# A chunked attention's scores and weighted sums in 64-row by 64-column tiles of TensorE, with its first loads in another order

## The chip, the cores and the metric

One core of one Trainium2 chip runs the whole kernel. The metric is the device time of one execution in microseconds (us). The core's engines are named as the profile names them: PE (TensorE matmuls), PEld (TensorE weight loads, which overlap PE), DVE (VectorE), ACT (ScalarE), POOL (GpSimd) and SP (SyncE, which here only issues transfers).

## The reference

Attention inside chunks of 64 tokens (8 batches, 8 heads, 576 tokens, 64 dimensions a head), then two stages over the 4608 tokens by 512 columns that come out: a mixture of 8 experts of which each token takes one, and a dense two-layer block. All data are float32.

```python
scores = scale * np.matmul(q_c, k_c.transpose(0, 1, 2, 4, 3))   # chunks of 64 tokens
scores = scores - np.max(scores, axis=-1, keepdims=True)
attn = np.exp(scores)
attn = attn / (np.sum(attn, axis=-1, keepdims=True) + 1e-09)
out = np.matmul(attn, v_c)
...
expert_idx = np.argmax(logits, axis=1)                          # logits = x @ w_gate
h = np.maximum(xe @ w1[e], 0.0)
out[mask] = gate_w[mask, None] * (h @ w2[e])
...
h = np.maximum(x @ w_in, 0.0)
return h * h @ w_out
```

## The kernel before

Three stages follow one another on PE: attention(), experts() and second(). The change is in attention() alone.

Attention works on 36 units of 128 tokens (two chunks of 64). A loop over `it` from -4 to 36 is software-pipelined, and everything is issued in the order in which it is written; each engine runs its own instructions in that order. In one iteration stand, for units that lie one to four apart: scores(it+1), the transposes of half of a q or k tile (trans, first half), x_t (transposes an older result), expo(it+1), trans (second half), pv(it-1), attn_t(it), and in some iterations the steps that choose the expert of each token: gate, gate_t with route, place, scatter, one in each of four iterations in turn.

- trans: PE turns q (even iterations) or k (odd ones) into PSUM tiles `tq`, and ACT copies them out in eight pieces of 64 partitions (four for each half) into `qT` or `kb`. The head's 64 dimensions lie on 64 partitions, so two heads (j = 0 and 1) fill 128. Before the change `kb` holds, for each pair of heads and each chunk, 2 x 64 columns: head 0's keys on partitions 0 to 63 in the first 64 columns, head 1's on partitions 64 to 127 in the last 64, and zeros elsewhere, written once at the start (fill_k, DVE).
- scores: eight matmuls (four pairs of heads, two chunks c2), each with 128 rows, 64 columns of weights (`lhsT`) and 128 moving columns, half of which meet the zeros. The two chunks write PSUM partitions 0 to 63 and 64 to 127. DVE then takes the maximum (`mx`) and subtracts it (`at`); ACT exponentiates (expo).
- attn_t transposes `at` on PE (`ta`), and ACT copies it out (`aT`). pv multiplies by v: again eight matmuls with 128 rows, 64 weight columns, and 130 moving columns of `vb`, which holds v of two heads side by side, with zeros and a column of ones for the sum (fill_v: on DVE for the first batch's set of buffers, on POOL for the second's). DVE divides (`rc`, `x`), and SP stores `x`.
- load_qk(u) loads q and k of two units (four chunks) on SP's queue, three u ahead of the k that has just been transposed; load_v(b) loads a batch of v on POOL's queue, for the first batch on both. A transfer on either queue waits until the transfer eight before it has landed, beside what its buffer needs.
- PSUM has eight banks: four tiles `t` that the transposes share, two score tiles `s` of a bank each, and one tile `v` of two banks.
- The buffers of tag "a" hold qk tiles (and, before, one `vb`), those of tag "b" hold kb, qT (and one `vb`), those of tag "h" the other `vb`; the experts use the same tags later for their weights.

A matmul of float32 data stands in the profile as two weight loads and two matmul records; a transpose as one of each.

Of the kernel before, what the change touches and what calls it, by code (L numbers as in the profile page):

```python
# [8 lines left out]
F32 = mybir.dt.float32  # L9
# [4 lines left out]
ALU = mybir.AluOpType  # L14
AX = mybir.AxisListType
PSUM = bass.MemoryType.PSUM
# [4 lines left out]
def kernel(ctx, tc, q, k, v, w_gate, w1, w2, w_in, w_out, out):  # L21
    nc = tc.nc
    B, H, S, D = q.shape
    NT, DM = out.shape
    NE = w_gate.shape[1]
    CH = 64
    NCB = S // CH
    NPAIR = H // 2
# [81 lines left out]
    at = const.tile([128, NI, QT], I32, name="at")  # L110
# [118 lines left out]
    def attention():  # L229
        with ExitStack() as actx:  # L230
            ps_t = actx.enter_context(tc.tile_pool(name="ps_t", bufs=4, space=PSUM))
            ps_s = actx.enter_context(tc.tile_pool(name="ps_s", bufs=2, space=PSUM))
            ps_v = actx.enter_context(tc.tile_pool(name="ps_v", bufs=1, space=PSUM))

            vb = [[tl("hhhhhhba"[4 * s + p], [128, NCB, 2, D + 1], F32, f"vb{s}{p}") for p in range(NPAIR)] for s in range(2)]
            kb = [tl("b", [128, NPAIR, 4, 2, CH], F32, f"kb{s}") for s in range(2)]
            st = {}

            def load_qk(u):
# [15 lines left out]
            def load_v(b, engs=(nc.gpsimd,), c0=0, c1=NCB):  # L255
                for p in range(NPAIR):
                    for j in range(2):
                        engs[j % len(engs)].dma_start(  # L258
                            out=vb[b % 2][p][64 * j:64 * j + 64, c0:c1, j, 0:D],
                            in_=v[b, 2 * p + j, CH * c0:CH * c1].rearrange("(c s) d -> s c d", s=CH),  # L260
                        )

            def trans(nm, u, hh):
                if hh == 0:
                    if nm == "q":
                        st["qT", u] = tl("b", [128, NPAIR, 128, 2], F32, f"qT{u}")
                src = st[nm, u] if hh == 0 else st.pop((nm, u))
                ps = ps_t.tile([128, 2, 2, 128], F32, tag="t", name="tq")
                for h in range(4):
                    nc.tensor.transpose(ps[:, h // 2, h % 2, :], src[:, 4 * hh + h, :], ident)  # L270
                for r in range(2):
                    for j in range(2):
                        i_ = ps[64 * r:64 * r + 64, :, j, :]
                        if nm == "q":
                            o = st["qT", u][64 * j:64 * j + 64, 2 * hh:2 * hh + 2, :, r]
                        else:
                            i_ = i_.rearrange("p a (c i) -> p a c i", c=4)
                            o = kb[u % 2].rearrange("p a c j (i r) -> p a j c i r", r=2)[64 * j:64 * j + 64, 2 * hh:2 * hh + 2, j, :, :, r]
                        nc.scalar.copy(o, i_)  # L279

            def scores(i):
                u, h2 = divmod(i, 2)
                qt, kt = st["qT", u], kb[u % 2]
                ps = ps_s.tile([128, H, CH], F32, tag="s", name="sc")
                for p in range(NPAIR):
                    for c2 in range(2):
                        c = 2 * h2 + c2
                        nc.tensor.matmul(
                            ps[64 * c2:64 * c2 + 64, 2 * p:2 * p + 2, :],
                            lhsT=qt[:, p, 32 * c:32 * c + 32, :].rearrange("p i r -> p (i r)"),  # L290
                            rhs=kt[:, p, c],
                            start=True,
                            stop=True,
                        )
                mx = tl("m", [128, H], F32, "mx")
                nc.vector.tensor_reduce(mx, ps, axis=AX.X, op=ALU.max)
                at = tl("r", [128, H, CH], F32, "at")
                nc.vector.tensor_tensor(out=at, in0=ps, in1=mx[:, :, None].to_broadcast([128, H, CH]), op=ALU.subtract)
                st["at", i] = at

            def expo(i):
                at = st["at", i]
                nc.scalar.activation(out=at, in_=at, func=AF.Exp, scale=scale)
# [10 lines left out]
            def pv(i):  # L314
                aT = st.pop(("aT", i))
                ps = ps_v.tile([128, 2, 512], F32, tag="v", name="pv")
                for p in range(NPAIR):
                    for c2 in range(2):
                        b, c = divmod(2 * i + c2, NCB)
                        o = (p % 2) * 2 * (D + 1)  # L320
                        nc.tensor.matmul(  # L321
                            ps[64 * c2:64 * c2 + 64, p // 2, o:o + 2 * (D + 1)],
                            lhsT=aT[:, p, 64 * c2:64 * c2 + 64],
                            rhs=vb[b % 2][p][:, c].rearrange("p j d -> p (j d)"),
                            start=True,
                            stop=True,
                        )
                pv_ = ps[:, :, 0:4 * (D + 1)].rearrange("p a (h d) -> p a h d", d=D + 1)
                rc = tl("m", [128, 2, 4, 1], F32, "rc")
                nc.vector.tensor_scalar(out=rc, in0=pv_[:, :, :, D:D + 1], scalar1=1e-9, scalar2=None, op0=ALU.add)  # L330
                nc.vector.reciprocal(out=rc, in_=rc)
                x = tl("x", [128, 2, 4, D], F32, "x")
                nc.vector.tensor_tensor(out=x, in0=pv_[:, :, :, 0:D], in1=rc.to_broadcast([128, 2, 4, D]), op=ALU.mult)
                nc.sync.dma_start(out=x_d[128 * i:128 * i + 128, :], in_=x.rearrange("p a h d -> p (a h d)"))
                st["x", i] = x

# [32 lines left out]
            nc.vector.memset(zero, 0)  # L369
            nc.scalar.dma_start(out=tk_d.rearrange("(e r) k -> e r k", e=NE)[:, 0, :], in_=zero)  # L370


            def fill_k(s):
                t = kb[s]
                nc.vector.memset(t[0:64, :, :, 1, :], 0.0)
                nc.vector.memset(t[64:128, :, :, 0, :], 0.0)

            def fill_v(s, eng):
                for t in vb[s]:
                    eng.memset(t[0:64, :, 1, :], 0.0)  # L380
                    eng.memset(t[64:128, :, 0, :], 0.0)
                    eng.memset(t[0:64, :, 0, D:D + 1], 1.0)
                    eng.memset(t[64:128, :, 1, D:D + 1], 1.0)

            fill_k(0)
            load_qk(1)
            c = min(6, NCB)
            load_v(0, (nc.gpsimd, nc.sync), 0, c)
            load_qk(2)
            if c < NCB:  # L390
                load_v(0, (nc.gpsimd, nc.sync), c)
            fill_v(1, nc.gpsimd)
            load_v(1)

            todo = {}
            for i in range(NTILE - 2):
# [6 lines left out]
            for g in range(NG - 1):  # L403
                t = 4 * g + (7 if g < NG - 3 else 6)
# [12 lines left out]
            for it in range(-4, NTILE + 1):  # L417
                u, h2 = divmod(it + 4, 2)
                tr = it + 4 < NTILE
                if 0 <= it + 1 < NTILE:  # L420
                    scores(it + 1)
                if tr:
                    trans("qk"[h2], u, 0)
                for step, i in todo.get(it, ()):
                    step(i)
                if 0 <= it + 1 < NTILE:
                    expo(it + 1)
                if tr:
                    trans("qk"[h2], u, 1)
                    if h2 == 1 and u + 3 < NUNIT:  # L430
                        load_qk(u + 3)
                if it == -4:
                    fill_k(1)
                if it == -3:
                    fill_v(0, nc.vector)
                if it == -1:
                    constants()
                if 0 <= it - 1 < NTILE:
                    pv(it - 1)
                    lo, hi = (2 * (it - 1)) // NCB, (2 * (it - 1) + 2) // NCB  # L440
                    if hi > lo and lo + 2 < B:
                        load_v(lo + 2)
                if 0 <= it < NTILE:
                    attn_t(it)
                late_steps(it)
                if it == NTILE - 14:
                    for _ in range(4):
                        load_next(most=1)
                if NTILE - 5 <= it < NTILE - 2:
                    split(1, 0, it - NTILE + 5, eng=nc.gpsimd)  # L450
# [599 lines left out]
    with tc.manual_schedule():  # L1050
        attention()
        experts()
        second()
# [30 lines left out]
```

## Time and profile before

| | |
|---|---|
| median of 3 runs | 1479.04 us (1475.89 to 1479.36) |
| the profiled execution | 1477.98 us, of which the span from first to last instruction is 1476.2 |
| PE busy | 1429.1 us, 97% of the span |
| attention, until the last weighted sum | 0 to 200 us |
| experts | to 690 us |
| second | to 1476 us |

The profiled execution lies 1.06 us under the median. PE's share is one of busy records: matmuls are pipelined and the profile models their ends, so a busy PE isn't PE at its peak. The rows further down are of one profiled execution. In a row of the timeline stand the start, the duration (both in us), the engine, the line of the kernel, what was done with which tiles and shapes and how many instructions the row merges; in brackets, how long the engine was idle before it and what ended that.

### The profile page before, as it was taken

How to read it: one execution, taken by the hardware profiler on the slowest of the kernel's cores; microseconds unless marked ns; L12 is line 12 of the kernel's file. 1: busy time of each engine (PE TensorE's matmuls, PEld its weight loads, DVE VectorE, ACT ScalarE, POOL GpSimd, SP SyncE). 2: the span in 40 equal slices, each digit the busy share in tenths (PEclk: the TensorE clock that was granted, in tenths of full speed). 3: DMA queues.
4: the chain of work that ended last, by engine and by line, in shares of the span. 5: the costliest groups of instructions: out<-in, count | busy, mean ns of one | idle time of the engine just before them, and what ended most of it. 6: DMA issues, size and time to landing. Idle time of an engine off the chain costs nothing.

```text
span 1476.2 us, 21686 instructions
## 1 busy us (share of the span) xinstructions
PE 1429.1 (97%) x8186; PEld 1219.6 (83%) x8186; DVE 757.4 (51%) x1374; ACT 601.0 (41%) x1111; POOL 468.7 (32%) x566
## 2 busy tenths in 40 slices
PE   6999978999999999999999999999999999999998
PEld 5777758888889999998888888888888888888886
DVE  4766767768887878885532232322233232322322
ACT  7988833443444445554432222222222222222222
POOL 5335455435545545653003040120403003040201
PEclk9999999999999999999999999999999999999999
DMA  9998645757767777885301010010101001010000
GB/s 202 262 216 208 171 130 183 217 171 228 235 210 232 238 229 256 260 269 179 107 1 59 0 60 0 24 36 0 59 0 52 8 8 52 1 59 1 30 2 29
DMA packets 144370, 172.91 MB, mean 117 GB/s; under 512 B 18160, under 2 KB 103872, under 8 KB 144256
## 3 DMA queue, kind: packets, MB, share of 16 engines
q1 hardware_dynamic: 110032, 112.58, 27.0%
q0 software_dynamic: 17920, 40.51, 9.8%
q10 hardware_dynamic: 16304, 18.36, 3.8%
q8 instruction: 66, 1.08, 0.3%
q14 instruction: 48, 0.39, 0.1%
HBM read 133.05 MB, written 38.34 MB: 116 GB/s over the span
## 4 chain that ended last, share of the span: by engine, by line
PE 53%; POOL 0%; POOLq 0%; issue 0%; DVE 0%
PE hp L993 27%; PE py L1014 26%; POOL out_dram L974 0%; POOLq L1079 0%; DVE o L1022 0%; POOL between L973 0%
## 5 line engine op out<-in xcount | busy, mean ns | idle before, releaser
L993 PE MATMUL hp<-xm,w_None 128*128 128x512 f32 x1728 | 416.5, 390 | 3.1 <-DVEq L937 3.1
L993 PEld LDWEIGHTS hp<-xm,w_None 128*128 128x128 f32 x1728 | 325.4, 188 | 71.0 <-ACTq L937 3.3
L1014 PE MATMUL py<-w_None,h 128*128 128x512 f32 x1512 | 363.2, 389 | 0.0
L1014 PEld LDWEIGHTS py<-w_None,h 128*128 128x128 f32 x1512 | 283.9, 188 | 58.8
L998 DVE SCALAR_TENSOR_TENSOR rs<-hp,rs 128x512 f32<-128x512 f32 x144 | 99.6, 691 | 435.0 <-ACT rs L997 431.6
L997 ACT ACTIVATE rs<-hp 128x512 f32<-128x512 f32 x144 | 85.9, 597 | 456.6 <-PE hp L993 446.0
L755 PE MATMUL pa<-xs,w 128*128 128x256 f32 (+2 forms) x1344 | 242.5, 329 | 6.9 <-DVE h L759 2.9
L767 PE MATMUL pb<-h,w 128*128 128x256 f32 (+2 forms) x1344 | 243.9, 331 | 0.0
L974 POOL DMA_INDIRECT out_dram<-o,tp x36 | 35.1, 974 | 628.6 <-ACT o L1020 622.6
L755 PEld LDWEIGHTS pa<-xs,w 128*128 128x128 f32 x1344 | 211.4, 189 | 24.7 <-DVE h L759 4.1
L767 PEld LDWEIGHTS pb<-h,w 128*128 128x128 f32 x1344 | 209.9, 190 | 14.5
L1000 DVE TENSOR_TENSOR h<-rs,h 128x512 fp32r<-128x512 f32 x144 | 99.7, 693 | 99.0 <-ACT h L999 95.5
L758 ACT ACTIVATE h<-pa 128x256 fp32r<-128x256 f32 (+2 forms) x112 | 53.2, 475 | 217.6 <-PE pa L755 169.9
L190 DVE TENSOR_TENSOR w<-raw,w 128x1024 fp32r<-128x1024 f32 x100 | 132.7, 1328 | 17.2 <-ACT w L189 12.4
L999 ACT CAST h<-rs 128x512 fp32r<-128x512 f32 x144 | 89.4, 621 | 111.2 <-DVE rs L998 100.2
L189 ACT CAST w<-raw 128x1024 fp32r<-128x1024 f32 x113 | 118.2, 1047 | 0.0
L759 DVE SCALAR_TENSOR_TENSOR h<-pa,h 128x256 fp32r<-128x256 f32 (+2 forms) x112 | 59.6, 535 | 61.5 <-ACT h L758 49.9
L803 POOL TENSOR_TENSOR cr<-cr 128x256 f32<-128x256 f32 x64 | 50.2, 784 | 124.5 <-ACT h L758 43.3
L804 POOL TENSOR_TENSOR cr<-cr 128x256 f32<-128x256 f32 x64 | 71.5, 1117 | 5.0
L258 POOL DMA_DIRECT2D vb<-in_v_dram x64 | 46.4, 747 | 67.4 <-PE pv L321 67.3
L270 PE MATMUL tq<-ident,qk 128*128 128x128 f32 x288 | 47.7, 296 | 14.1 <-DMA qk<-in_q_dram 9.9
L279 ACT COPY qT<-tq 64x256 f32<-64x256 f32 x144 | 56.0, 389 | 10.8 <-PE tq L270 9.1
(197 smaller groups left out, 1316.0 us busy)
## 6 DMA issues: line engine op xcount, KB each, us to landing
raw<-in_moe_w_dram SPq DMA_DIRECT2D x112, 512.0 KB
x_d<-x SPq DMA_DIRECT2D x36, 256.0 KB
x<-y_d POOLq DMA_DIRECT2D x36, 256.0 KB
cr<-in_moe_w_in_dram SPq DMA_DIRECT2D x32, 256.0 KB
cr<-in_moe_w_out_dram SPq DMA_DIRECT2D x32, 256.0 KB
vb<-in_v_dram POOLq DMA_DIRECT2D x56, 144.0 KB
qk<-in_q_dram SPq DMA_DIRECT2D x12, 512.0 KB
qk<-in_k_dram SPq DMA_DIRECT2D x12, 512.0 KB
```

Of the source, the lines that this page charges most:

```text
L189: nc.scalar.copy(w[0], raw)
L190: eng.tensor_tensor(out=w[1], in0=raw, in1=w[0], op=ALU.subtract)
L755: nc.tensor.matmul(ps[:, 0:N], lhsT=w[wl][:, kk, o:o + 128], rhs=xT[:, xl, kk, 0:N], start=(kk == 0 and wl + xl == 0), stop=(kk == KD - 1 ...
L759: nc.vector.scalar_tensor_tensor(out=h[:, 1, 0:N], in0=ps[:, 0:N], scalar=0.0, in1=h[:, 0, 0:N], op0=ALU.max, op1=ALU.subtract)
L767: nc.tensor.matmul(pb[d][:, 0:N], lhsT=w[wl][:, f % 2, 128 * d:128 * d + 128], rhs=h[:, hl, 0:N], start=(f + hl + wl == 0), stop=(f == NF ...
L804: nc.gpsimd.tensor_tensor(out=af, in0=af, in1=ef, op=ALU.add)
L993: nc.tensor.matmul(ps, lhsT=w[wl][:, kk, o:o + 128], rhs=xT[:, xl, kk, :], start=(kk == 0 and wl + xl == 0), stop=(kk == KD - 1 and wl == 1))
L997: nc.scalar.activation(out=rs[:, 0], in_=ps, func=AF.Relu)
L998: nc.vector.scalar_tensor_tensor(out=rs[:, 1], in0=ps, scalar=0.0, in1=rs[:, 0], op0=ALU.max, op1=ALU.mult)
L999: nc.scalar.copy(h[:, 0], rs[:, 1])
L1000: nc.vector.tensor_tensor(out=h[:, 1], in0=rs[:, 1], in1=h[:, 0], op=ALU.subtract)
L1014: nc.tensor.matmul(ys[t], lhsT=h[:, hl, 128 * t:128 * t + 128], rhs=w[wl][:, g % 2, :], start=(g == 0 and hl + wl == 0), stop=(g == NF2 - ...
```

## The change

`kb` and `vb` lose their zeros: keys and values of head j lie on partitions 64j to 64j+63 and nothing else does. Each score or weighted-sum matmul of 128 rows becomes two of 64 rows (j = 0, 1), which read 64 partitions each and write different PSUM banks, with 64 (65) moving columns instead of 128 (130). The score tile takes two banks and has one buffer where it had two of one bank. The `vb` tiles are four instead of eight and all have tag "h", so that "a" has a fourth buffer for qk and "b" a third for qT. The zero fills go; only columns of ones are written, by POOL, at the start. The first batch of v is loaded in chunks 0 to 1 and 2 to 8 (before 0 to 5 and 6 to 8), the first piece before the second q and the rest behind the third k; load_v(1) is written in iteration 0 instead of before the loop.

```diff
-            ps_s = actx.enter_context(tc.tile_pool(name="ps_s", bufs=2, space=PSUM))
+            ps_s = actx.enter_context(tc.tile_pool(name="ps_s", bufs=1, space=PSUM))
...
-            vb = [[tl("hhhhhhba"[4 * s + p], [128, NCB, 2, D + 1], F32, f"vb{s}{p}") for p in range(NPAIR)] for s in range(2)]
-            kb = [tl("b", [128, NPAIR, 4, 2, CH], F32, f"kb{s}") for s in range(2)]
+            vb = [[tl("h", [128, 2, NCB, D + 1], F32, f"vb{s}{z}") for z in range(NPAIR // 2)] for s in range(2)]
+            kb = [tl("b", [128, NPAIR, 128, 2], F32, f"kb{s}") for s in range(2)]
...
-                            out=vb[b % 2][p][64 * j:64 * j + 64, c0:c1, j, 0:D],
+                            out=vb[b % 2][p // 2][64 * j:64 * j + 64, p % 2, c0:c1, 0:D],
...
+                to = st["qT", u] if nm == "q" else kb[u % 2]
                 for r in range(2):
                     for j in range(2):
...
-                        nc.scalar.copy(o, i_)
+                        nc.scalar.copy(to[64 * j:64 * j + 64, 2 * hh:2 * hh + 2, :, r], ps[64 * r:64 * r + 64, :, j, :])
...
-                ps = ps_s.tile([128, H, CH], F32, tag="s", name="sc")
+                ps = ps_s.tile([128, 2, 512], F32, tag="s", name="sc")
                 for p in range(NPAIR):
                     for c2 in range(2):
-                        c = 2 * h2 + c2
-                        nc.tensor.matmul(
-                            ps[64 * c2:64 * c2 + 64, 2 * p:2 * p + 2, :],
-                            lhsT=qt[:, p, 32 * c:32 * c + 32, :].rearrange("p i r -> p (i r)"),
-                            rhs=kt[:, p, c],
...
+                        for j in range(2):
+                            c = slice(64 * h2 + 32 * c2, 64 * h2 + 32 * c2 + 32)
+                            nc.tensor.matmul(
+                                ps[64 * c2:64 * c2 + 64, j, CH * p:CH * p + CH],
+                                lhsT=qt[64 * j:64 * j + 64, p, c].rearrange("q i r -> q (i r)"),
+                                rhs=kt[64 * j:64 * j + 64, p, c].rearrange("q i r -> q (i r)"),
...
-                        nc.tensor.matmul(
-                            ps[64 * c2:64 * c2 + 64, p // 2, o:o + 2 * (D + 1)],
-                            lhsT=aT[:, p, 64 * c2:64 * c2 + 64],
-                            rhs=vb[b % 2][p][:, c].rearrange("p j d -> p (j d)"),
...
+                        for j in range(2):
+                            nc.tensor.matmul(
+                                ps[64 * c2:64 * c2 + 64, j, (D + 1) * p:(D + 1) * (p + 1)],
+                                lhsT=aT[64 * j:64 * j + 64, p, 64 * c2:64 * c2 + 64],
+                                rhs=vb[b % 2][p // 2][64 * j:64 * j + 64, p % 2, c],
...
-            fill_k(0)
+            for s_ in range(2):
+                for t in vb[s_]:
+                    nc.gpsimd.memset(t[:, :, :, D:D + 1], 1.0)
+            load_v(0, (nc.gpsimd, nc.sync), 0, 2)
             load_qk(1)
-            c = min(6, NCB)
-            load_v(0, (nc.gpsimd, nc.sync), 0, c)
             load_qk(2)
-            if c < NCB:
-                load_v(0, (nc.gpsimd, nc.sync), c)
-            fill_v(1, nc.gpsimd)
-            load_v(1)
+            load_v(0, (nc.gpsimd, nc.sync), 2)
...
-                if it == -4:
-                    fill_k(1)
-                if it == -3:
-                    fill_v(0, nc.vector)
+                if it == 0:
+                    load_v(1)
```

On PE, one iteration in the middle of attention before (from one call of scores to the next; `tq` is a half of trans, `tx` x_t, `ta` attn_t):

```order
L288 MATMUL sc<-kb_115,qT_1244 64x128 x8
L270 MATMUL tq<-ident,qk_1047 128x128 x4
L348 MATMUL tx<-ident,x 128x128 x4
L270 MATMUL tq<-ident,qk_1047 128x128 x4
L321 MATMUL pv<-vb_110,aT 64x130 x2
L321 MATMUL pv<-vb_111,aT 64x130 x2
L321 MATMUL pv<-vb_112,aT 64x130 x2
L321 MATMUL pv<-vb_113,aT 64x130 x2
```

and such an iteration of the changed kernel:

```order
L286 MATMUL sc<-kb_111,qT_1440 64x64 x16
L271 MATMUL tq<-ident,qk_1374 128x128 x4
L348 MATMUL tx<-ident,x 128x128 x4
L271 MATMUL tq<-ident,qk_1374 128x128 x4
L321 MATMUL pv<-vb_108,aT 64x65 x8
L321 MATMUL pv<-vb_109,aT 64x65 x8
L309 MATMUL ta<-ident,at 128x128 x4
L286 MATMUL sc<-kb_110,qT_1620 64x64 x16
```

Nothing has moved; scores and pv have sixteen matmuls of half the moving columns where they had eight.

On POOL's queue at the start, before (vb_106 to vb_109 are the first batch's buffers, vb_110 to vb_113 the second's; a DMASW semaphore tells that the transfer eight earlier has landed):

```order
L258 DMA vb_106<-in_v_dram 64x3x64
L258 DMA vb_107<-in_v_dram 64x3x64
L258 DMA vb_108<-in_v_dram 64x3x64
L258 DMA vb_109<-in_v_dram 64x3x64 [waits DMASW0_49]
L380 MEMSET vb_110 64x9x65
L381 MEMSET vb_110 64x9x65 [waits Pool_49]
...
L383 MEMSET vb_113 64x9
L258 DMA vb_110<-in_v_dram 64x9x64 [waits DMASW1_49]
```

and in the changed kernel (vb_106 and vb_107 are the first batch's, vb_108 and vb_109 the second's):

```order
L374 MEMSET vb_109 128x18
L259 DMA vb_106<-in_v_dram 64x2x64 x2
L259 DMA vb_107<-in_v_dram 64x2x64 x2
L259 DMA vb_106<-in_v_dram 64x7x64 x2
L259 DMA vb_107<-in_v_dram 64x7x64
L259 DMA vb_107<-in_v_dram 64x7x64 [waits DMASW0_49]
L259 DMA vb_108<-in_v_dram 64x9x64 [waits DMASW1_49]
L259 DMA vb_108<-in_v_dram 64x9x64 [waits DMASW2_49]
```

The second batch's loads, though written in iteration 0, stand directly behind the first batch's on POOL and wait for nothing but the transfers eight before them; sixteen memsets that stood between are gone.

## Rows read from the trace of the kernel before

**Rows 1.** The page, section 1: busy us, share of the span, instructions.

```profile
PE 1429.1 (97%) x8186; PEld 1219.6 (83%) x8186; DVE 757.4 (51%) x1374; ACT 601.0 (41%) x1111; POOL 468.7 (32%) x566
```

**Rows 2.** Windows, four stretches: each engine's busy us (instructions), PE clock, DMA share, GB/s.

```profile
0.00:12.46 12.46, 5.69 (x25) 4.71 (x25) 8.62 (x21) 7.01 (x16) 11.06 (x29) 1.00 0.93 192
12.46:35.42 22.96, 15.81 (x142) 12.84 (x141) 7.73 (x22) 17.61 (x44) 7.49 (x15) 0.85 1.20 207
35.42:186.25 150.83, 142.32 (x1598) 110.94 (x1597) 106.01 (x264) 132.14 (x307) 64.94 (x98) 1.00 0.89 213
186.25:212.00 25.75, 15.92 (x135) 11.34 (x135) 14.68 (x35) 6.60 (x11) 12.87 (x17) 0.93 0.46 140
```

**Rows 3.** Groups on ACT, 35.42 to 186 us: busy us, mean ns, idle before them.

```profile
L279 ACT COPY kb<-tq 64x256 f32<-64x256 f32 x120 | 46.7, 389 | 1.4
L279 ACT COPY qT<-tq 64x256 f32<-64x256 f32 x116 | 45.2, 390 | 5.1 <-PE tq L270 3.8
L303 ACT ACTIVATE at<-at 128x512 f32<-128x512 f32 x31 | 19.5, 631 | 5.5 <-DVE at L298 4.6 <-ACT kb L279 0.3
L311 ACT COPY aT<-ta 128x512 f32<-128x512 f32 x31 | 18.1, 585 | 3.7 <-PE tq L270 3.0
L358 ACT COPY gs<-gl 128x512 f32<-128x512 f32 x7 | 4.1, 591 | 1.2 <-PE tx L348 0.9 <-PE tq L270 0.4
```

**Rows 4.** ACT's waits, 35.42 to 186 us: us in total, times, longest.

```profile
ACT at L303 <- DVE at L298: 4.6, 6, 1.5
ACT qT L279 <- PE tq L270: 3.8, 4, 1.0
ACT aT L311 <- PE tq L270: 3.0, 2, 1.6
ACT gs L358 <- PE tx L348: 0.9, 1, 0.9
ACT gs L358 <- PE tq L270: 0.4, 1, 0.4
```

**Rows 5.** Timeline of one iteration in the middle, PE and PEld.

```profile
48.35 0.85 PEld L288 LDWEIGHTS sc<-kb,qT 128*64 128x64 f32 x16 [0.17 <-issue]
48.35 1.09 PE L288 MATMUL sc<-kb,qT 128*64 128x128 f32 x16
...
51.01 1.11 PE L321 MATMUL pv<-vb,aT 128*64 128x130 f32 x16
...
52.63 0.42 PEld L288 LDWEIGHTS sc<-kb,qT 128*64 128x64 f32 x8 [0.17 <-issue]
```

**Rows 6.** Line 356, a gate step: ns min/median/max, first and last start.

```profile
L356 PE MATMUL gl<-xT,wg x8: 592/604/617, 57.0 to 57.5; 128*32 128x512 f32 x8
```

**Rows 7.** Timeline of the start: the third k arrives, and what follows.

```profile
27.56 1.56 PE L270 MATMUL tq<-ident,qk 128*128 128x128 f32 x8 [3.40 <-DMA qk<-in_k_dram]
...
28.36 1.59 ACT L279 COPY kb<-tq 64x256 f32<-64x256 f32 x4 [2.95 <-PE tq L270]
...
33.46 1.58 ACT L279 COPY qT<-tq 64x256 f32<-64x256 f32 x4 [0.60 <-PE tq L270]
```

**Rows 8.** Groups of the start, 0 to 20 us: two of the zero fills.

```profile
L380 POOL MEMSET vb<- 64x585 f32 x4 | 2.4, 590 | 0.2
...
L375 DVE MEMSET kb<- 64x1024 f32 x2 | 1.8, 912 | 0.4 <-issue 0.4
```

**Rows 9.** Timeline of an iteration in which POOL scatters.

```profile
95.99 1.09 PE L288 MATMUL sc<-kb,qT 128*64 128x128 f32 x16
...
97.57 0.99 POOL L510 DMA_INDIRECT tk_d<-tok,pos  x1 [0.23 <-issue]
...
98.33 0.69 DVE L296 TENSOR_REDUCE mx<-sc 128x8 f32<-128x512 f32 x1 [2.68 <-PE tx L348]
...
99.08 0.38 ACT L279 COPY qT<-tq 64x256 f32<-64x256 f32 x1 [1.05 <-PE tq L270]
```

**Rows 10.** Timeline of the end of attention, DVE.

```profile
201.24 0.17 DVE L330 TENSOR_SCALAR rc<-pv 128x8 f32<-128x8 f32 x1 [4.01 <-remote]
```

More of the change, by code (lines that the diff above doesn't have):

```diff
@@ L270, in trans @@
                     nc.tensor.transpose(ps[:, h // 2, h % 2, :], src[:, 4 * hh + h, :], ident)
+                to = st["qT", u] if nm == "q" else kb[u % 2]
                 for r in range(2):
                     for j in range(2):
[L273 to L278, printed above, removed]
-                        nc.scalar.copy(o, i_)
+                        nc.scalar.copy(to[64 * j:64 * j + 64, 2 * hh:2 * hh + 2, :, r], ps[64 * r:64 * r + 64, :, j, :])
             def scores(i):
@@ L283, in scores @@
                 qt, kt = st["qT", u], kb[u % 2]
-                ps = ps_s.tile([128, H, CH], F32, tag="s", name="sc")
+                ps = ps_s.tile([128, 2, 512], F32, tag="s", name="sc")
                 for p in range(NPAIR):
                     for c2 in range(2):
-                        c = 2 * h2 + c2
-                        nc.tensor.matmul(
-                            ps[64 * c2:64 * c2 + 64, 2 * p:2 * p + 2, :],
-                            lhsT=qt[:, p, 32 * c:32 * c + 32, :].rearrange("p i r -> p (i r)"),
-                            rhs=kt[:, p, c],
[L292 to L296, printed above, removed]
+                        for j in range(2):
[4 more added lines that the diff above has]
+                                rhs=kt[64 * j:64 * j + 64, p, c].rearrange("q i r -> q (i r)"),
+                                start=True,
+                                stop=True,
+                            )
+                s4 = ps[:, :, 0:NPAIR * CH].rearrange("q j (p k) -> q j p k", k=CH)
+                mx = tl("m", [128, 2, NPAIR], F32, "mx")
+                nc.vector.tensor_reduce(mx, s4, axis=AX.X, op=ALU.max)
                 at = tl("r", [128, H, CH], F32, "at")
-                nc.vector.tensor_tensor(out=at, in0=ps, in1=mx[:, :, None].to_broadcast([128, H, CH]), op=ALU.subtract)
+                nc.vector.tensor_tensor(out=at.rearrange("q (p j) k -> q j p k", j=2), in0=s4,
+                                        in1=mx[:, :, :, None].to_broadcast([128, 2, NPAIR, CH]), op=ALU.subtract)
                 st["at", i] = at
@@ L319, in pv @@
                         b, c = divmod(2 * i + c2, NCB)
-                        o = (p % 2) * 2 * (D + 1)
-                        nc.tensor.matmul(
-                            ps[64 * c2:64 * c2 + 64, p // 2, o:o + 2 * (D + 1)],
-                            lhsT=aT[:, p, 64 * c2:64 * c2 + 64],
-                            rhs=vb[b % 2][p][:, c].rearrange("p j d -> p (j d)"),
[L325 to L328, printed above, removed]
+                        for j in range(2):
[3 more added lines that the diff above has]
+                                rhs=vb[b % 2][p // 2][64 * j:64 * j + 64, p % 2, c],
+                                start=True,
+                                stop=True,
+                            )
+                pv_ = ps[:, :, 0:4 * (D + 1)].rearrange("q j (p d) -> q j p d", d=D + 1)
                 rc = tl("m", [128, 2, 4, 1], F32, "rc")
@@ L331, in pv @@
                 nc.vector.reciprocal(out=rc, in_=rc)
-                x = tl("x", [128, 2, 4, D], F32, "x")
-                nc.vector.tensor_tensor(out=x, in0=pv_[:, :, :, 0:D], in1=rc.to_broadcast([128, 2, 4, D]), op=ALU.mult)
+                x = tl("x", [128, 4, 2, D], F32, "x")
+                nc.vector.tensor_tensor(out=x.rearrange("q p j d -> q j p d"), in0=pv_[:, :, :, 0:D], in1=rc.to_broadcast([128, 2, 4, D]), op=ALU.mult)
                 nc.sync.dma_start(out=x_d[128 * i:128 * i + 128, :], in_=x.rearrange("p a h d -> p (a h d)"))
@@ L370, in attention @@
             nc.scalar.dma_start(out=tk_d.rearrange("(e r) k -> e r k", e=NE)[:, 0, :], in_=zero)
[L373 to L383, printed above, removed]
-            fill_k(0)
+            for s_ in range(2):
+                for t in vb[s_]:
+                    nc.gpsimd.memset(t[:, :, :, D:D + 1], 1.0)
+            load_v(0, (nc.gpsimd, nc.sync), 0, 2)
             load_qk(1)
-            c = min(6, NCB)
-            load_v(0, (nc.gpsimd, nc.sync), 0, c)
             load_qk(2)
-            if c < NCB:
-                load_v(0, (nc.gpsimd, nc.sync), c)
-            fill_v(1, nc.gpsimd)
-            load_v(1)
+            load_v(0, (nc.gpsimd, nc.sync), 2)
             todo = {}
```

## The prediction

> **What bounds the kernel now.** The page comes first: PE is busy for 97% of the span [rows 1]. That is a mean over three stages, and the change lies in the first, so the second view is the table of windows over attention alone [rows 2]. It cuts attention at calls of scores: the start, until the fifth call at 35.42 us; the regular middle, 31 calls until 186.25 us; and the end, until the experts' matmuls fill PE at 212 us. The start is bound by transfers: PE is busy for 15.8 of 23.0 us, while the DMA engines' share is 1.20 at 207 GB/s. In the middle PE and ACT are both nearly full: 142.3 and 132.1 of 150.8 us. PE's figure contains modelled ends, ACT's does not, so I read the middle from ACT: an iteration takes 150.83 / 31 = 4.87 us, and ACT works in it for 132.14 / 31 = 4.26 us. The groups on ACT say with what [rows 3]: eight copies of 0.39 us, the exponential, the copy of `aT` and, in one iteration of four, `gs`. None of them gets shorter by this change.
>
> ACT is idle for 18.7 us of the middle. Its list of waits names 12.7 us of that in 14 waits [rows 4]: 8.1 us in eight that PE ended (3.8 + 3.0 + 0.9 + 0.4) and 4.6 us in six that DVE's subtraction ended, which itself follows scores. The other 6 us lie in gaps of 10 to 20 ns between instructions (18.7 less 12.7, over 307 instructions, is 20 ns each). So whatever PE saves in the middle, at most about 12.7 us can come out of the stage.
>
> **The change on PE.** A scores call now issues 16 records, whose weight loads take 0.85 us, and takes 1.09 us with its latency; pv takes 1.11 us [rows 5]. 0.85 / 8 is 106 ns for two records: the two chunks write different column halves, and their records run as a pair. That more than two can run at once is shown by the gate, with four tiles of 32 columns: its eight records of some 600 ns all start within 0.5 us, 57.0 to 57.5 [rows 6]. That is two rounds of four, the second 0.5 us or less behind the first, for 512 moving columns; the 106 ns for 128 fits the same pace. So time goes with moving columns, and tiles in different columns run together.
>
> The changed calls have 32 records each, in four tiles (two row halves, two column halves), of 64 or 65 moving columns. If all four run together, that is 8 rounds of half of 106 ns, 0.42 us instead of 0.85: 0.42 us less for each call, 0.84 us in an iteration. If the row halves don't run side by side, it is 16 rounds of 53 ns, 0.85 us as now. If in addition a record keeps the 53 ns that it has now on average, however few columns it has, 32 records take 1.70 us. No row shows two row halves at once, so both ends stay open; I take the first, since the gate shows four tiles in flight, which is the nearest row.
>
> **What that is worth, stage by stage.** *Middle.* An iteration of PE, from one scores call to the next, took 4.28 us, 48.35 to 52.63 [rows 5], near ACT's 4.26, so PE's 0.84 us is at first only a lead over ACT. It is worth something where ACT waits. Between two such waits PE does one scores and one pv, so each of the eight waits that PE ends can shrink by 0.84 us at most: four of 3.8 us in all, the longest 1.0, give 3.4; two of 3.0 give 1.7; 0.8 and 0.4 come from `gs`; together 6.3 us. The six that wait for DVE's subtraction shrink by the earlier scores alone, 0.42 us each, 2.5 us. The most is 8.8 us. The least is nothing, for a reason that the rows show (first rival, below). Between the two I take half, 4.4 us.
>
> *Start.* PE waits 3.40 us for the third k, until 27.56 us, and ACT 2.95 us behind it [rows 7]. Before that k has to come, before: three q and three k of 0.52 MB, 0.98 MB of the first v (SP's last quarter MB of v is behind it), and the second batch of v, 1.18 MB; now 0.13 MB of SP's v instead of 0.39 is ahead, the rest stands behind. The second v isn't held back: on POOL nothing stands between it and the first, it even comes earlier by the fills that are gone. So 0.26 MB less, at 207 GB/s [rows 2], is 1.25 us; the q that comes next (ACT's copies of it start at 33.46 us) has the same bytes ahead as before, and stands 0.6 us behind ACT anyway. I take 1.2 us. The most is the whole wait, 3.4 us. The least: the second v, 5.7 us of transfers at that rate, gets ahead of the second k. Then ACT has that k's copies, an exponential, the third q's copies and `aT`, some 7.5 us of work, between about 20.7 and 28.2 us, and still reaches the third k's copies at 28.4, as now: nothing lost.
>
> *End.* The last pv is done before 199 us, but DVE begins its division at 201.24 us, after 4.01 us idle, released by nothing on PE [rows 10]. Three pv calls of 0.42 us lie ahead of it; I count 0, at most 1.3 us.
>
> *What costs nothing.* The zero fills: the largest groups take 2.4 us on POOL and 1.8 on DVE [rows 8], all before 14.4 us, while PE waits for loads; without that cover they would be worth some 5 us on either engine. The fourth qk and third qT buffers only take waits from SP and ACT that end behind the transfers and PE anyway. The single score buffer adds a wait: scores must follow DVE's subtraction of the call before, and the transposes behind it on PE, whose copies ACT needs, wait too. In a regular iteration the subtraction ends some 2 us before the next scores, which hides it; where scatters run it may not (a rival).
>
> **Sum.** 4.4 + 1.2 + 0 = 5.6 us off the profiled 1477.98, 1472.4. Experts and second are PE-bound behind attention and move up whole. The profiled execution was 1.06 us under the median, so the median should come to **1473 us**; its own range is 1465 to 1477.
>
> **Rivals.** *Scatters, not PE, make ACT's waits.* In the iteration at 96 us scores ends by its record at 97.08, yet DVE's maximum starts at 98.33 after 2.68 us idle, and ACT's copy at 99.08 after 1.05, while POOL issues its indirect scatters [rows 9]. PE's signals seem to come late there, and a faster PE wouldn't release them sooner. Against it: PE would enter such a stretch with more lead. Then only the start's 1.2 us remains, 1478. Chance 0.20.
>
> *The change doesn't do what it says*: row halves take turns, a call stays 0.85 us: 1478 again. 0.07.
>
> *Everything is collected*: 8.8 + 3.4 + 1.3 = 13.5 us, 1465. 0.07.
>
> *A record costs 53 ns whatever its size* (slower). Then two calls cost 2 x 0.85 us more in an iteration, PE needs about 4.28 + 1.70, some 6.0 us, and with a quarter of a gate step (1 us) 6.2, against 4.87: 1.35 x 31 = 42 us more, 1520. It decides as soon as an iteration of PE with its share of the gate passes 4.87 us, that is when the two calls grow by more than some 0.3 us. Chance 0.10. The Trainium skill has such a rule, in "TensorE: Matmul & The Clock Gate", "Step-by-step: what each phase is for": with hardware decoding off, the sequencer spends about 62 ns on each matmul, whatever it computes. By it the 80 matmul records of an iteration (64 for the two calls, 16 transposes) would take 4.96 us, an estimate, 0.1 us over the present iteration, and the time would be some 1482; the trace has 16 records in 0.85 us, 53 ns each, under that floor, though in short bursts. The skill's "TensorEngine Tiling (Array Packing)", "Instruction Overhead", warns likewise against tiling a dimension that is already small, with about 60 cycles as the floor of a matmul; 64 columns lie just above it, so by that rule the sum stays.
>
> *The single score buffer* (slower). Where scatters delay DVE, its subtraction ends late (in the iteration of rows 9 the maximum alone starts 1.25 us late), and now scores waits for it. If each of seven gate cycles loses 1.5 us and nothing is won, 10 us less the start's 1.2: 1488; if half of the 4.4 us is won, 1485. It decides where the subtraction ends more than 0.84 us after scores would otherwise start. Chance 0.08.
>
> **Chances and range.** The forecast has 0.48. What this kernel's runs tell from no change is about 0.3%, 4.4 us: faster is under 1474.6, slower over 1483.5. Of the forecast 0.38 falls under 1474.6 and 0.10 within; with 0.07 for everything collected, faster has 0.45; the two rivals at 1478 bring "same" to 0.37; the two slower ones make 0.18. The range 1464 to 1485 leaves out the 1520 and part of the two cases at its ends.
>
> **What would show it.** The profile after should have scores and pv rows of 32 records in about 0.65 us where they had 16 in 1.1; if they read 1.1 the row halves take turns, if 2 a record has a fixed price. ACT's busy time in the middle should stay near 4.26 us an iteration, its waits that PE ended fall from 8.1 towards 3 us, and the wait for the third k shrink by about 1 us, the second v landing earlier than before. DVE's idle time at the scatters tells whether these set the rest. The forecast is wrong if PE's clock, 1.00 in the whole middle [rows 2], fell to 1.2 GHz because PE now does less, or if DVE's operations on scores in two banks became longer.

## The result, and the profile after

The change made the kernel slower: 1489.7 us (median of 4, 1487.2 to 1490.9) against 1479.2 (4, 1475.9 to 1480.4), a ratio of 1.0072 with a 95% interval of 1.0051 to 1.0094. Forecast were 1473 us and a range of 1464 to 1485.

The page, section 1:

```profile
PE 1425.0 (96%) x9338; PEld 1215.8 (82%) x9338; DVE 752.0 (51%) x1354; ACT 600.7 (40%) x1111; POOL 465.4 (31%) x554
```

PE is busy for 4 us less than in [rows 1] with 1152 records more of each kind, and the span is 12.7 us longer. Two rows of the table of windows, cut at the same calls of scores as [rows 2] (the first, the fifth, the last):

```profile
11.57:36.95 25.38, 17.17 (x237) 14.21 (x237) 7.96 (x22) 19.03 (x48) 2.84 (x4) 0.60 1.18 201
36.95:196.37 159.42, 135.30 (x2589) 105.46 (x2589) 110.21 (x268) 131.54 (x306) 66.75 (x102) 0.91 0.82 204
```

The middle went from 150.83 to 159.42 us, 8.6 of the 12.7. ACT worked in it as long as before (131.54 against 132.14 us), PE 7 us less, and PE's clock, 1.00 throughout before, has a mean of 0.91. So nobody works more: somebody waits. The calls themselves did what was forecast. Timeline, two undisturbed calls, which answer to [rows 5], then a disturbed one and what follows it:

```profile
36.95 0.69 PE L286 MATMUL sc<-kb,qT 64*64 64x64 f32 x32
...
39.03 0.70 PE L321 MATMUL pv<-vb,aT 64*64 64x65 f32 x32
...
61.07 0.33 PE L321 MATMUL pv<-vb,aT 64*64 64x65 f32 x2
...
63.07 0.69 PE L321 MATMUL pv<-vb,aT 64*64 64x65 f32 x30 [1.67 <-issue]
...
65.34 1.14 PE L286 MATMUL sc<-kb,qT 64*64 64x64 f32 x32
...
67.56 1.61 ACT L275 COPY kb<-tq 64x256 f32<-64x256 f32 x4 [2.33 <-PE tq L271]
```

A row of the table of windows for the stretch behind the pause (PE's clock is the third number from the end):

```profile
63.99:67.41 3.42, 3.42 (x45) 2.97 (x44) 2.54 (x11) 1.20 (x3) 0.00 (x0) 0.50 0.40 109
```

A call takes 0.69 us where it took 1.1. But at 61 us PE stops after two of 32 records and goes on 1.67 us later; "issue" says that it waited for nothing that the profile shows. Behind that the clock is at half level (1.2 GHz) from 64.0 to 67.4 us, the next scores take 1.14 us, and ACT waits 2.33 us, longer than any of its waits in the middle before. A second such pause, 1.9 us in front of a transpose at 155 us, is followed by half clock from 156.2 to 159.6. Between 78 and 180 us there are five more places where PE's records come in pieces, a few at a time with gaps of 0.2 to 1.1 us, while POOL issues scatters; four of them, all but the one at 124 us, are followed by half clock too. PE's longest waits put down to issue, 44 to 180 us (us in total, times, longest):

```profile
PE sc L286 <- issue: 4.8, 9, 1.1
PE pv L321 <- issue: 4.2, 8, 1.7
```

With the transpose's 1.9 and three of 0.2 that is 11.5 us, where the profile before has a single wait of 0.3. The pauses at 61 and 155 us are 3.6 of them; some 7.5 lie in the five places.

ACT's waits in the middle, which answer to [rows 4], and two rows of the timeline of the end:

```profile
ACT at L303 <- DVE at L297: 9.2, 4, 3.9
ACT kb L275 <- PE tq L271: 5.9, 5, 2.3
ACT qT L275 <- PE tq L271: 4.2, 5, 1.7
ACT aT L311 <- remote: 4.0, 3, 1.7
ACT aT L311 <- PE ta L309: 0.6, 1, 0.6
```

```profile
186.57 2.34 DVE L464 TENSOR_TENSOR cm<-cm,c 128x8 bf16<-128x8 bf16 x1
...
190.39 1.13 PE L286 MATMUL sc<-kb,qT 64*64 64x64 f32 x32 [1.24 <-DVE at L297]
```

What PE ended is 10.7 us in eleven waits (8.1 in eight before), what DVE ended 9.2 (4.6); for 4.0 the view names no engine ("remote"). The single score buffer does bind at the end: scores at 190.39 wait for the subtraction, which comes late because DVE stood in a small addition for 2.34 us while POOL worked on a weight.

### The profile page after: what moved, and what is told of

The parts are those of the page before. It is cut to its first block, busy times and chain, and to the rows that moved or that the text cites. A ratio compares the mean times of both kernels' runs of the same rounds, so it can differ in the third digit from the quotient of the medians.

```text
span 1488.9 us, 23954 instructions
## 1 busy us (share of the span) xinstructions
PE 1425.0 (96%) x9338; PEld 1215.8 (82%) x9338; DVE 752.0 (51%) x1354; ACT 600.7 (40%) x1111; POOL 465.4 (31%) x554
## 4 chain that ended last, share of the span: by engine, by line
PE 52%; DMA 0%; POOL 0%; issue 0%; DVE 0%; POOLq 0%
PE py L997 26%; PE hp L976 26%; DMA x<-y_d 0%; POOL out_dram L957 0%; POOLq L1062 0%; POOL tp L941 0%; DVE o L1005 0%; DVE rs L981 0%; POOL raw L172 0%; POOL between L956 0%; POOLq L172 0%; POOLq L941 0%
## 5 line engine op out<-in xcount | busy, mean ns | idle before, releaser
L741 ACT ACTIVATE h<-pa 128x256 fp32r<-128x256 f32 (+2 forms) x112 | 53.2, 475 | 219.7 <-PE pa L738 174.7
L190 DVE TENSOR_TENSOR w<-raw,w 128x1024 fp32r<-128x1024 f32 x100 | 132.7, 1327 | 17.2 <-ACT w L189 12.7
L271 PE MATMUL tq<-ident,qk 128*128 128x128 f32 x288 | 54.6, 326 | 19.7 <-DMA qk<-in_q_dram 12.9
```

The costliest lines, as they stand in the source:

```text
L190: eng.tensor_tensor(out=w[1], in0=raw, in1=w[0], op=ALU.subtract)
```

## The experiments

Three theories: **R**, the doubled number of PE records costs, not their content; **C**, 64-row tiles by themselves lower the clock; and the parts that the prediction had priced: the load order, the single score buffer. In the groups of runs below the kernel before takes 1465 us, not 1479, so each ratio is to the kernel before of the same group. Ratios stand with their 95% intervals.

**The two halves of the change.** e1 is the kernel before with this edit alone:

```diff
-            load_qk(1)
-            c = min(6, NCB)
-            load_v(0, (nc.gpsimd, nc.sync), 0, c)
-            load_qk(2)
-            if c < NCB:
-                load_v(0, (nc.gpsimd, nc.sync), c)
+            load_v(0, (nc.gpsimd, nc.sync), 0, 2)
+            load_qk(1)
+            load_qk(2)
+            load_v(0, (nc.gpsimd, nc.sync), 2)
             fill_v(1, nc.gpsimd)
-            load_v(1)
...
+                if it == 0:
+                    load_v(1)
```

> Matmuls, buffers and zero fills as in the kernel before; only the order of the first loads is the changed kernel's (v in chunks 0 to 1 and 2 to 8, the second batch of v behind them, called in iteration 0). Theory A, the new load order by itself delays the start (the third q and k land later, ACT is 0.8 us later at the fifth exponential in the changed kernel): 0.5 to 2 us slower than before, 1480 to 1481. Theory B, the start is lost only because TensorE runs at half clock from 19.6 to 36.7 us in the changed kernel, and that comes with the small matmuls: here the half-clock stretches stay those of before (21 to 25, 28 to 31 us) and the time is within 1 us of before or up to 1.2 us better, 1478 to 1479.

Measured: 0.9999 (0.9990 to 1.0009). The load order alone is worth nothing that this run can tell.

e2 is the changed kernel with the old order (load_v of chunks 0 to 5 behind load_qk(1), 6 to 8 behind load_qk(2), load_v(1) behind that).

> The changed kernel's matmuls, buffers and single score tile, with the first loads in the order of the kernel before (the zero fills stay away). Theory A (load order costs): about 1 us better than the changed kernel, 1488 to 1489. Theory B (the small matmuls cost): the same as the changed kernel within 1 us, with half-clock stretches in the middle of attention again, and pauses of some 2 us inside a call without any wait.

Measured: 1.0037 (1.0027 to 1.0047). So the loss lies in the matmuls, as theory B says; the longest pauses without a wait are 3.3 us in front of a transpose at 147 us and 1.5 in scores at 110.

**Records without small tiles; the score buffer.** e3 is the kernel before, with two matmuls in place of one:

```diff
-                            ps[64 * c2:64 * c2 + 64, 2 * p:2 * p + 2, :],
+                            ps[64 * c2:64 * c2 + 64, 2 * p + j, :],
...
-                            rhs=kt[:, p, c],
+                            rhs=kt[:, p, c, j],
```

and the same in pv (65 of the 130 columns each).

> The kernel before, with each of its score and weighted-sum matmuls split in two by moving columns: 16 matmuls (32 records) a call as in the changed kernel, 64 or 65 moving columns each, but 128 rows with the zeros, two score buffers and the loads of before. Theory R (the number of records costs: the instruction stream runs dry at a block's end, and while POOL scatters few records pass): pauses of about 2 us without a wait inside calls in the middle, as at 61 and 153 us of the changed kernel, and a time 4 to 9 us over before, 1483 to 1488. Theory C (the 64-row tiles leave the clock at half level): the clock stays 1.00 in the whole middle and the time is within 2 us of before, 1478 to 1481. Forecast's rival that a record has a fixed price: a call takes 1.7 us or more.

Measured: 1.0051 (1.0033 to 1.0069). A call, then the longest of PE's waits put down to issue, 44 to 180 us (us in total, times, longest):

```profile
147.71 1.20 PE L289 MATMUL sc<-kb,qT 128*64 128x64 f32 x32
```

```profile
PE tx L350 <- issue: 1.8, 1, 1.8
PE rank L493 <- issue: 0.7, 1, 0.7
```

With 128 rows and all zeros in place the loss is there, the pauses too, and half clock (152.2 to 155.6) behind the longer one: theory C isn't needed for them. The rival of a fixed price of 53 ns a record is out: 32 records take 1.20 us, against 1.09 for 16. But here PE also works 1.2 us for a call, and the start lost some 3 us (fifth exponential at 43.8 us, 40.9 in e6), so 0.51% isn't all pauses.

e4 is the changed kernel with `sc2 = ps_s.tile([128, 2, 2, 256], ...)` made once and `ps = sc2[:, :, i % 2]` in scores.

> The changed kernel with two score buffers that share the two banks (columns 0 to 255 and 256 to 511 of each), so that scores need not follow the subtraction of the call before. Theory S (the single score buffer costs at the end of attention, where DVE is held up and scores of 190.4 and 196.4 us wait for the subtraction): 3 to 6 us better than the changed kernel, 1484 to 1487, most of it after 182 us. Theory R or C (records or the clock): the end hardly changes, 1488 to 1490.

Measured: 1.0033 (1.0017 to 1.0049), against 1.0037 and 1.0040 with one buffer: no difference that these runs can tell.

**Where the pauses stand.** e5 and e6 are the two kernels themselves.

> The changed kernel once more, on the chip of this group, beside the kernel before. Theory R (the stream of PE instructions runs dry at the end of every 256th, when the block's fetch comes late): pauses of 1 to 3.5 us without a wait at PE's records 1473, 3009, 3265, 3521, 3777 or 4545, the places of the runs with 32 records a call, and a half-clock stretch a few us behind the longer ones; 0.3 to 0.7% over before. Theory D (what was lost on the first chip, 0.7%, came mostly from PE passing few records while POOL scatters): if such pauses don't appear here, as they did not in the last four runs, the loss is 0.3 to 0.4%.

> The kernel before on the chip of this group, for its profile. Theory R: no pause of over 0.6 us without a wait at any multiple of 256 records; the clock 1.00 in the middle. Theory D: the start of DVE's maximum within 0.1 us of the end of scores nearly everywhere, no waits of 1 us and more behind POOL's scatters, and attention some 10 us shorter than in the first profile of this kernel.

Measured: the changed kernel 1.0040 (1.0029 to 1.0051). Its waits put down to issue, 44 to 180 us, are seven, the longest 2.6 us; the kernel before (e6) and its variants with 16 records a call (e1, e7, e11, e14) have none. The table of windows of e5, cut inside each of these pauses (PE, PEld, DVE, ACT, POOL):

```profile
PE sc L286 <- issue: 4.5, 2, 2.6
PE tq L271 <- issue: 3.9, 2, 2.5
PE pv L321 <- issue: 3.8, 2, 2.6
PE tx L348 <- issue: 2.1, 1, 2.1
```

```profile
46.99:54.00 7.01, 5.27 (x126) 4.34 (x126) 4.10 (x9) 6.80 (x17) 5.05 (x7) 1.00 1.14 289
54.00:62.00 8.00, 6.66 (x125) 4.88 (x125) 4.75 (x9) 6.90 (x17) 0.76 (x2) 1.00 1.09 248
62.00:106.00 44.00, 37.37 (x753) 28.22 (x753) 31.76 (x84) 39.11 (x94) 20.31 (x32) 0.96 0.88 214
106.00:114.00 8.00, 5.37 (x126) 4.47 (x126) 5.32 (x14) 7.24 (x18) 2.48 (x4) 1.00 1.06 244
114.00:124.00 10.00, 7.45 (x125) 5.61 (x124) 4.52 (x8) 7.13 (x17) 7.78 (x14) 0.83 1.04 214
124.00:152.00 28.00, 24.68 (x502) 19.21 (x503) 21.50 (x58) 24.02 (x57) 10.72 (x17) 0.94 0.86 207
```

Add PE and PEld: 252, 250, 1506, 252, 249 and 1005 instructions, that is 1, 1, 6, 1, 1 and 4 times 251. With PE's semaphore instructions, which these rows leave out, the trace counts exactly 256, 256, 1536, 256, 256 and 1024. Any two of the pauses lie a multiple of 256 instructions apart, wherever in the program that falls: pv, scores, a transpose. In the first profile the two pauses are 3072 apart, 12 times 256. What comes in such pieces is PE's program: section 3 of the page has a queue of kind "instruction" with packets of 16 KB. Its row, after and before:

```profile
q8 instruction: 74, 1.21, 0.4%
q8 instruction: 66, 1.08, 0.3%
```

The DMA queues (packets, MB, share of 16 engines), 53.3 to 60.4 us and 60.4 to 61.8 us of the first profile, between the crossing from one piece to the next at 53.2 and the pause at 61.2:

```profile
q0 software_dynamic: 447, 0.99, 66.8%
q1 hardware_dynamic: 773, 0.77, 37.4%
...
```

```profile
q1 hardware_dynamic: 820, 0.41, 107.7%
q8 instruction: 1, 0.02, 5.1%
...
```

The piece that PE needs next isn't moved for 7 us, then at the last moment, and PE stands until it has it. The trace's packet records say the same of e5: before each of the seven pauses the packet starts 4.1 to 6.8 us after PE crossed into the piece before, and PE goes on 1.3 to 1.6 us after it has landed; where a packet lands 2 us or more before PE needs it, PE doesn't stop. In the kernel before (e6) a piece lasts PE 10 us and more, in e5 6 to 10. In e6 packets land up to 7.5 us after the crossing, nearly as late as here (8.0 us), but still 3.3 us or more before they are needed, so the delay is hidden there and isn't here.

e6 took 1466.6 us, a single run. Its scatters don't hold DVE up, unlike [rows 9]:

```profile
76.67 0.99 POOL L510 DMA_INDIRECT tk_d<-tok,pos  x1 [0.21 <-issue]
...
77.70 1.09 PE L288 MATMUL sc<-kb,qT 128*64 128x128 f32 x16
...
78.84 0.69 DVE L296 TENSOR_REDUCE mx<-sc 128x8 f32<-128x512 f32 x1 [1.48 <-PE sc L288]
```

The maximum starts 0.05 us behind scores. From 44 to 170 us ACT's listed waits are 0.8 us in e6, all told, and 13.2 in e5, 12.7 of them ended by PE: the pauses and the half clock reach ACT, and in a profile in which DVE doesn't wait behind scatters, the middle of the kernel before has next to nothing that a faster PE could win.

**Holding v back.** e7 is e1 with this edit (`hold` is one column in SBUF); e11 has it in the kernel before, with the old order of the first loads.

```diff
-                if it == 0:
-                    load_v(1)
+                if it == 1:
+                    nc.gpsimd.tensor_copy(hold, st["at", 2][:, 0, 0:1])
+                    load_v(1)
```

> The kernel before with the changed kernel's order of first loads, and the second batch of v really held back: POOL first copies one element a row of the third exponential's result, so that its transfers start at some 27 us. Theory H (the second batch of v, 1.18 MB, is what delays the third q and k at the start, about 5 us of ACT's waits in the run with the loads alone): 2 to 5 us faster than before, 0.1 to 0.35%. Theory N (the start is bound by the sum of the transfers, or the clock gives it back): no change within 1 us.

> The kernel before with its own order of first loads (v in chunks 0 to 5 and 6 to 8), and only the second batch of v held back in the same way. If holding it back is the whole gain: 0.994 to 0.997 of before. If the new order of the first loads is needed for it: 0.998 to 1.0.

Measured: e7 0.9955 (0.9939 to 0.9970), e11 0.9960 (0.9946 to 0.9973). Timeline of e6 at the start, then of e7:

```profile
14.33 5.84 POOL L258 DMA_DIRECT2D vb<-in_v_dram  x8
...
33.32 1.94 PE L270 MATMUL tq<-ident,qk 128*128 128x128 f32 x8 [5.26 <-DMA qk<-in_q_dram]
...
34.45 1.56 ACT L279 COPY qT<-tq 64x256 f32<-64x256 f32 x4 [4.86 <-PE tq L270]
```

```profile
26.62 0.18 POOL L435 COPY hold<-at 128x1 f32<-128x1 f32 x1 [12.09 <-ACT at L304]
27.09 5.85 POOL L259 DMA_DIRECT2D vb<-in_v_dram  x8 [0.28 <-issue]
...
29.26 1.58 ACT L280 COPY qT<-tq 64x256 f32<-64x256 f32 x4 [0.56 <-PE tq L271]
```

ACT's wait of 4.86 us for the fourth q becomes 0.56. Both beat the kernel before, by 5.8 and 5.6 us of the medians (2 to 5 were expected of e7), and the changed kernel by more; the order of the first loads adds nothing that these runs can tell.

**Half the records; less data; small tiles with held loads.** e8 has scores as e4 and pv as before, e12 pv as the changed kernel and scores as before, both with the changed load order. e9 leaves `load_v(lo + 2)` out of the changed kernel. e10 is e4 with the held loads of e7.

> Scores as in the changed kernel (64-row tiles, 32 records, two buffers in the two banks), weighted sums as before (16 records), the loads in the changed order. Theory R: half of the added records, so the blocks of instructions last longer and fewer run dry: one or two pauses over 1 us in place of five, 0 to 0.2% over before. Theory C (64-row tiles by themselves lower the clock): half-clock stretches in the middle without a pause ahead of them, 0.2 to 0.4% over before.

> Weighted sums as in the changed kernel (64-row tiles, 32 records, v without zeros), scores as before (16 records, two buffers, k with zeros), the loads in the changed order. Theory R (the count of records, not which call has them): like the run with small scores alone, pauses of under 1 us at the ends of blocks and 0.998 to 1.002 of before. If it lies in one kind of call: 1.003 or more here, since the small scores alone cost nothing.

> The changed kernel without the loads of v's third to eighth batch (its six last batches are weighted by v of the first two), so that POOL issues no transfers of v after the start; one look, since other tokens choose other experts. Theory R with the reason that a block of PE instructions comes late because the data transfers stand ahead of its own: pauses over 0.6 us at multiples of 256 records shrink from five to eight, some 9 to 17 us in all, to at most two. Rival: the fetch is late by itself (PE takes the blocks too fast): the pauses stay, five or more.

> The changed kernel with two score buffers in its two banks and with the second batch of v held back by POOL's copy of one element a row of the third exponential. Theory R: the held loads give the start 3 to 5 us, as with the old matmuls, and the pauses of the 32-record calls take 3 to 6 us in the middle: within 0.2% of before, and 0.25 to 0.5% behind the run with the old matmuls and held loads (0.9955). Rival: with the start in order the small tiles are worth something: as fast as that run or faster, 0.993 to 0.996.

Measured: e8 0.9995 (0.9982 to 1.0008), e12 0.9998 (0.9985 to 1.0010), e10 1.0006 (0.9992 to 1.0020). e9 took 2045.5 us, a single run, almost all of the excess behind attention, where other tokens chose other experts; its attention alone is of use. PE's waits put down to issue, 44 to 180 us, of e8, of e12, of e9 and of e10:

```profile
PE tq L272 <- issue: 0.5, 1, 0.5
PE sc L287 <- issue: 0.4, 1, 0.4
```

```profile
PE tq L274 <- issue: 1.4, 1, 1.4
PE sc L293 <- issue: 0.6, 1, 0.6
PE pv L326 <- issue: 0.3, 1, 0.3
```

```profile
PE pv L321 <- issue: 0.9, 2, 0.6
PE sc L286 <- issue: 0.7, 1, 0.7
```

```profile
PE sc L288 <- issue: 3.5, 2, 2.0
PE pv L323 <- issue: 2.9, 1, 2.9
PE tx L350 <- issue: 2.8, 1, 2.8
...
```

With half of the added records the pauses shrink to 2.3 us or less and the loss is gone, whichever call has them; e8 has no pause over 1 us, where one or two were expected, and e12 has one of 1.4 us, where under 1 was expected. Without POOL's later loads the full 32-record calls keep 1.6 us of pauses. With the loads held, small tiles lose to e7 by 0.5%: they are worth less than nothing, as theory R said.

**Which transfers are in the way.** e13 is e10, and e14 is e7, with `load_v(lo + 2, (nc.sync,))`: the same bytes on SP's queue.

> The run with small tiles, two score buffers and held loads, with v's third to eighth batch loaded by SP's queue (in line with q, k and the stores of x) in place of POOL's. If it is the packets of POOL's queue that stand ahead of the blocks of PE instructions: at most two pauses of over 0.6 us, as in the run without those loads, and 4 to 7 us faster than with POOL's queue, 0.995 to 0.998 of before. If any transfer does it: the same pauses as with POOL's queue, six of 11 us in all, and 1.000 to 1.003.

> The same change of queue for the kernel before with held loads (matmuls as before), which has no such pauses: what v on SP's queue does by itself. Expected: within 0.15% of that run, 0.994 to 0.998 of before; slower if the loads of v, which wait for a weighted sum, hold up q and k behind them on SP.

Measured: e13 0.9978 (0.9966 to 0.9989), e14 1.0007 (0.9997 to 1.0016). In e13 one wait of issue is left, 44 to 180 us:

```profile
PE tg L444 <- issue: 1.3, 1, 1.3
```

So it is mostly the packets of POOL's queue that delay the pieces of PE's program, and not the amount of data alone. SP's transfers can do it too: in e9 a piece of PE's program starts to move 5.2 us after PE's crossing at 39.9 us and PE pauses for 0.6 us at 47.4, while the queues from 39.9 to 46.5 us show SP's transfers and that piece alone:

```profile
q1 hardware_dynamic: 3055, 1.91, 114.1%
q8 instruction: 1, 0.02, 1.2%
```

Small tiles almost without pauses (e13) reach the experts' first matmul at 190.6 us, e14 at 191.0, e7 at 190.8: alike. The miss is e14, 0.5% behind e7: its last instruction ends as early as e7's (1453.35 against 1453.54 us), but the span goes on for 9.6 us behind it, in e7 for 3.7. e13 has 9.6 us there as well, so its 0.9978 holds some 6 us that aren't attention's. The rows show nothing in that time. The trace's records of instructions that the rows leave out have one that lasts through most of it, a drain with which POOL ends its program: 9.9 us in e13 and e14, 4.0 in e7, and the other engines' last signals come behind it. Why it takes longer there is open.

## Why the prediction was wrong

- *The calls* were right: 0.69 us where "about 0.65" was said; the row halves run side by side, and ACT's busy time stayed.
- *The middle* failed, and with it the sign. The step was "The least is nothing": a faster call was taken to leave, at worst, everything as it was. Eight more matmuls in each of the two calls also are 64 more instructions an iteration, and only the time that they run was priced, not their way to PE. The pauses where a piece of 256 instructions arrives late, with the half clock behind the long ones, made the kernel 0.37 to 0.40% slower (e2, e5), some 5 to 6 us, in place of the 4.4 us that were to be won. How the loss divides between the pauses and the clock wasn't separated.
- *The gain of the middle* had been read from ACT's waits of [rows 4]. The rival that scatters make these waits is borne out as far as two profiles of one kernel can show it: in e6, where the scatters don't hold DVE up, the waits are gone (0.8 us to 170 us), and so is the gain; e13, free of most pauses, is no faster in attention than e7.
- *The start*, -1.2 us: the order is worth 0.9999 in e1, an interval of some 1.4 us either way, so the term isn't refuted. In the first comparison the fifth call of scores came 1.5 us later, at 36.95 us, with PE's clock at a mean of 0.60 ahead of it. The sentence before it was the useful one: "The second v isn't held back". Holding it was worth 5.6 to 5.8 us (e7, e11), more than the 3.4 that I had named as the whole wait.
- *The single score buffer*, given 0.08 with 1485 to 1488, comes nearest to the time but isn't the cause: two buffers don't help (e4). In the first profile it did bind at 190 and 196 us.
- *A price for each record whatever its size* had the right sign by the wrong mechanism: 32 records take 0.69 us, 22 ns each. In e3 a record takes 37 ns. The rule of the Trainium skill weighed there ("TensorE: Matmul & The Clock Gate", "Step-by-step: what each phase is for"), some 62 ns for each matmul where hardware decoding is off, doesn't show in these rows.
- *The clock* was named as what would make the forecast wrong, and it did fall, but not because of shorter calls: in e8 and e12, where one of the two calls is short, it is at full level from 44 us to the last calls of scores, and in e9, where both are, from 44 to 172 us.
- *Open:* 0.72% in the first comparison, 0.40% in e5. The first profile has what no later one has: pieces of calls while POOL scatters, some 7.5 us of PE's waits, and DVE held up at 186 us. e6's attention is also shorter than that of the first profile before the change, by as much as its whole time is. No later run shows this, so its cause and its share stay open.

## What to carry to other kernels

Count instructions as well as time: where a stage issues some 256 PE instructions in 7 us while POOL's queue moves data, twice the matmuls of half the size can cost more than they save, as here, and an idle put down to issue at a fixed distance in instructions is the sign of it. Before a busy engine is made faster, look at what the other engines wait for in a profile without disturbances. A load that is written later isn't issued later: give its queue something to wait for.

## What the hardware showed that was not expected

- PE's program comes in pieces of 256 instructions, 16 KB in one packet of a queue of its own, and PE stood up to 3.3 us (e2) at the seam between two pieces when the packet was late. The Trainium skill, "Runtime: NRT & Kernel Launch", "Instruction fetch mechanics", says the same of the pieces; that the cost of a seam is "mostly hidden" holds here where both calls have 16 records, and not where both have 32.
- In the 7.1 us ahead of the first pause POOL's queue took 66.8% of 16 engines for 447 packets of some 2.2 KB, 170 ns a packet; SP's 37.4% for 773 of 1.0 KB, 55 ns. The same bytes on SP's queue leave the seams almost quiet (e13).
- Two row halves and two column halves of TensorE run at once: 32 records of 64 rows in 0.69 us, against 1.20 us for 32 of 128 rows (e3).
